# Attention with top-k MLP on one core: dense output rows, query tiles of 1024 columns, and values' products five blocks behind the scores

## The chip, the cores and the metric

One core of a Trainium2 chip runs the program. The metric is the device time of one execution in microseconds, as the median of several runs. TensorE (PE) multiplies matrices, VectorE (DVE), ScalarE (ACT) and GpSimd (POOL) do the elementwise work, and SyncE (SP) issues nearly all transfers to 16 DMA engines.

## The reference

For each of four batches there are 12288 queries of 128 channels. The keys, which are the values too, are 384 x 32 positions averaged over 4 x 4 windows, which leaves 768, and multiplied by a 128 x 128 matrix. Softmax attention follows. On its output `x` a gate picks the 128 rows of a batch with the highest score, and these rows alone get a small MLP added.

```python
kv_pool = kv.reshape(B, H // r, r, W // r, r, C).mean(axis=(2, 4))
k = v = kv_pool.reshape(B, -1, C) @ w_sr
s = (q @ k.transpose(0, 2, 1)) / sqrt(C)
a = exp(s - s.max(-1)); a /= a.sum(-1) + 1e-09
x = a @ v
scores = x @ w_gate                          # one score for a row
top = argpartition(-scores[b], 128)[:128]
out[b, top] = x[b, top] + sigmoid(scores[b, top]) * (relu(x[b, top] @ w1) @ w2)
```

## The kernel before, in words

The loop of lines 602 to 646 goes over 192 blocks of 256 queries, 48 for a batch. Each query of a block is split into a high and a low part, each probability too, so that products in fast formats keep the precision.

Iteration `i` does this. `s_max(i)` (L338) takes the maximum of block i's scores in PSUM on DVE. `AV` (L374) multiplies the turned probabilities of block `i - LAG`, with `LAG` 4, by the values: 36 matmuls of 130 columns, of which 128 are the value, one is the sum of the probabilities and one the gate's score. `S(i + 1)` (L326) makes the next block's scores in 12 matmuls, in the other of two PSUM buffers. `exp` and `to_high` on ACT and `to_low` on DVE and POOL write the block's probabilities to the tile `hl`, a half in fp16 and a half in bf16. `turn(i, 0)` and `turn(i, 1)` (L371) have the DMA engines transpose the two halves into the tile `at`, one DMA for each. `sums`, `recip` and `finish` (L385 to L409) normalise block `i - LAG` on DVE out of the one PSUM tile `o_two`, which the next AV overwrites. `hl` has 4 buffers and `at` has 5.

`finish` multiplies all 130 columns by the reciprocal into the tile `x` (2 blocks, 4 rows of 130 floats in a partition). After each second block POOL copies the gate's column out of `x` to the scores (L406), and SP writes the 128 others to HBM (L408). The four rows lie next to each other in HBM but 130 floats apart in SBUF, so a row of 512 bytes is a piece of its own.

Queries come in through `load_q` (L129): a tile holds 2048 columns (8 blocks), there are two such tiles, and each DMA brings the 512 columns of two blocks, 256 KB. `split_q` (L314) reads the columns two iterations before their scores. `next_keys` (L256) prepares the next batch's keys beside a batch: it loads 1 MB a key tile in two DMAs of 512 KB and sums on POOL. In the last batch there is nothing to prepare. `topk` (L411) and `pick` (L456) select the rows and run the MLP of the batch before, a step at a time at fixed points of the loop.

PE, DVE, ACT and POOL run in the order in which the Python code issues (`InOrder`, L39). SP's DMAs run in one order too, but the scheduler chooses it, and a load stands in it as early as its tile is free. SP's order in the trace repeats every 8 blocks: two transposes a block, an output after each second block, and four query loads, of which three stand next to each other right after a tile of queries has been split for the last time. Key loads come between, alone or in twos.

After the loop (L647 to L735) the last four blocks' products follow, and the last batch's selection and MLP run with nothing beside them.

Of the kernel before, what the change touches and what calls it, by code (L numbers as in the profile page):

```python
# [6 lines left out]
F32 = mybir.dt.float32  # L7
# [7 lines left out]
ALU = mybir.AluOpType  # L15
# [4 lines left out]
P = 128  # L20
B, N, C = 4, 12288, 128
# [4 lines left out]
CHUNK = 2048  # L26
JPC = CHUNK // P
NCH = N // CHUNK
QT = 2
BLK = QT * P  # L30
NBLK = N // BLK
BPC = CHUNK // BLK
VC = C + 2
NCOL = N // P
CUT = 2 * M - HALF
# [29 lines left out]
def attention_topk_mlp(ctx, tc, a, outs, capacity):  # L65
    nc = tc.nc
    pe, dve, act, pool = (InOrder(tc, e) for e in (nc.tensor, nc.vector, nc.scalar, nc.gpsimd))
# [3 lines left out]
    kvp = ctx.enter_context(tc.tile_pool(name="kvp", bufs=3))  # L71
    kvs = ctx.enter_context(tc.tile_pool(name="kvs", bufs=2))
    keys = ctx.enter_context(tc.tile_pool(name="keys", bufs=2))
    qp = ctx.enter_context(tc.tile_pool(name="qp", bufs=2))
    qs = ctx.enter_context(tc.tile_pool(name="qs", bufs=3))
    wk = ctx.enter_context(tc.tile_pool(name="wk", bufs=3))
    hlp = ctx.enter_context(tc.tile_pool(name="hlp", bufs=4))
    at = ctx.enter_context(tc.tile_pool(name="at", bufs=5))
    ob = ctx.enter_context(tc.tile_pool(name="ob", bufs=3))
    sm = ctx.enter_context(tc.tile_pool(name="sm", bufs=4))  # L80
    tk = ctx.enter_context(tc.tile_pool(name="tk", bufs=2))
# [18 lines left out]
    o_two = ps_o.tile([P, QT, 512], F32, name="o_two")  # L100
    o_all = o_two[:, :, 0:VC]
    banks = [o_two[:, j] for j in range(QT)]
# [23 lines left out]

    qraw = {}

    def load_q(b, ch, lo=0, hi=CHUNK):  # L129
        if (b, ch) not in qraw:  # L130
            qraw[b, ch] = qp.tile([P, CHUNK], F32, name="q_raw")
        nc.sync.dma_start(out=qraw[b, ch][:, lo:hi], in_=a["q"][:, b, ch, lo:hi])

    kvset = {}

    def new_keys(b):
        kvset[b] = {
            "kh": keys.tile([P, M], F32R, name="kh"),
            "kl": keys.tile([P, M], F32R, name="kl"),
            "raw": keys.tile([P, KT, 2, P], F32, name="kv_proj"),  # L140
            "vw": keys.tile([P, KT], F32, name="vw"),
            "mx": keys.tile([P, 4], F32, name="mx"),
            "vx": keys.tile([P, 2, KT, VC], F16, name="vx"),
            "sg": keys.tile([P, 4], F32, name="sg"),
        }

    def project(pooled, ps):
        pe.matmul(ps[:, 0], w_k, pooled, start=True, stop=True)
        pe.matmul(ps[:, 1], pooled, w_sr, start=True, stop=True)
# [24 lines left out]
    def v_split(b):  # L174
# [18 lines left out]
        dve.tensor_scalar(out=sg[:, 3:4], in0=sg[:, 0:1], scalar1=float(TAPS), scalar2=None, op0=ALU.mult)  # L193
        vw3, col = vw.rearrange("p (t o) -> p t o", o=1), slice(C + 1, VC)
        act.activation(vw3, vw3, AF.Copy, scale=sg[:, 1:2])
# [14 lines left out]
    def first_keys():  # L210
        new_keys(0)
        load_q(0, 0, 0, 2 * BLK)
        raws = [load_kv(0, kc) for kc in range(3)]
        nc.sync.dma_start(out=cst, in_=a["cst"])
        raws += [load_kv(0, kc, 2) for kc in range(3, KT)]
        load_q(0, 0, 2 * BLK, CHUNK)
        split_q(0, 0)
        kv = kvset[0]
        for kc in range(KT):
            pooled = kvs.tile([P, P], F32, name="pooled")  # L220
            for h in range(2):
                dve.tensor_reduce(out=pooled[:, h * P // 2:(h + 1) * P // 2], in_=raws[kc][:, h], axis=AX.X, op=ALU.add)
            if kc == 4:
                dve.tensor_copy(tri16, tri)
            if kc > 1:
                v_gate(0, kc - 2)
            if kc == 3:
                v_max(0, 0)
            ps = banks[kc % 2][:, 0:2 * P].rearrange("p (a b) -> p a b", a=2)
            if kc < KT - 1:  # L230
                project(pooled, ps)
                act.copy(kv["raw"][:, kc], ps)
                split_k(0, kc, kc + 1, 0)
                split_k(0, kc, kc + 1, 1)
            else:
                warm(4, banks[0][:, 0:P])
                project(pooled, ps)
                kh, kl = (kv[k][:, kc * P:(kc + 1) * P] for k in ("kh", "kl"))
                dve.tensor_copy(kh, ps[:, 0])
                dve.tensor_tensor(out=kl, in0=ps[:, 0], in1=kh.bitcast(F32), op=ALU.subtract)  # L240
                act.copy(kv["raw"][:, kc, 1], ps[:, 1])
                warm(8, banks[1][:, 0:P])
        S(0)
        S(1)
# [64 lines left out]
    scores = {}  # L309
    qsplit = {}  # L310
    st = {}
    xt_ = {}

    def split_q(b, blk):  # L314
        ch, h = divmod(blk, BPC)
        raw = qraw[b, ch][:, h * BLK:(h + 2) * BLK]
        qh = qs.tile([P, 2 * BLK], F32R, name="qh")
        ql = qs.tile([P, 2 * BLK], F32R, name="ql")
        act.copy(qh, raw)
        pool.tensor_tensor(out=ql, in0=raw, in1=qh.bitcast(F32), op=ALU.subtract)  # L320
        for i in range(2):
            qsplit[b, blk + i] = qh[:, i * BLK:(i + 1) * BLK], ql[:, i * BLK:(i + 1) * BLK]

    blocks = [(b, blk) for b in range(B) for blk in range(NBLK)]
# [67 lines left out]
    def recip(n):  # L392
        dve.reciprocal(st[n]["rz"], st[n]["rz"])

    def finish(n):
        b, blk = blocks[n]
        o, rz = st[n]["o"], st[n]["rz"]
        if blk % 2 == 0:
            xt_[b] = ob.tile([P, 2 * QT, VC], F32, name="x")
        x = xt_[b]  # L400
        dve.tensor_tensor(out=x[:, (blk % 2) * QT:(blk % 2 + 1) * QT], in0=o, in1=rz.rearrange("p (j o) -> p j o", o=1).broadcast_to([P, QT, VC]), op=ALU.mult)
        if blk % 2:
            if blk == 1 and b not in scores:
                scores[b] = tk.tile([P, NCOL], F32, name="sc")
            if n < nb - 1:
                pool.tensor_copy(scores[b][:, (blk - 1) * QT:(blk + 1) * QT], x[:, :, C + 1])  # L406
            ch, h = divmod(blk // 2, BPC // 2)
            nc.sync.dma_start(out=outs[b].rearrange("(h p j) d -> h p j d", p=P, j=JPC)[ch, :, h * 2 * QT:(h + 1) * 2 * QT], in_=x[:, :, 0:C])  # L408
        del st[n]  # L409

    def topk(b):  # L411
# [165 lines left out]
    blocks = [(b, blk) for b in range(B) for blk in range(NBLK)]  # L577
# [20 lines left out]

    start(vals, first_values())
    nb = len(blocks)  # L600
    LAG = 4
    for i in range(nb):
        old = i >= LAG
        b, blk = blocks[i]
        if blk % 2 == 0 and i + BPC < nb:
            nb_, nblk = blocks[i + BPC]
            load_q(nb_, nblk // BPC, nblk % BPC * BLK, (nblk % BPC + 2) * BLK)
        if blk == 0 and b + 1 < B:
            start(prep, next_keys(b + 1))
        if i:  # L610
            borrow(s_flat[(i - 1) % 2], s_flat[(i - 1) % 2][:, 512:513])
        s_max(i)
        if old:
            AV(i - LAG, 0)
            at_point("pe")
            AV(i - LAG, 1)
        else:
            at_point("pe")
            warm(18 if i == 0 else 36, banks[0][:, 0:P])
        if i % 2 == 0 and i + 2 < nb:  # L620
            split_q(*blocks[i + 2])
        at_point("ev")
        at_point("up")
        at_point("t")
        at_point("cmp")
        at_point("g")
        if 0 < i < nb - 1:
            S(i + 1, (3, 2, 1, 0))
        exp(i, 1)
        exp(i, 2)  # L630
        to_high(i, 1)
        if old:
            sums(i - LAG)
            recip(i - LAG)
            finish(i - LAG)
        to_low(i, 1, dve)
        exp(i, 0)
        to_high(i, 0)
        turn(i, 0)
        to_low(i, 0, pool)  # L640
        turn(i, 1)
        at_point("d")
        if i in (1, 2):
            advance(vals, "d")
        if old and blocks[i - LAG][1] == NBLK - 1:
            start(select, topk(blocks[i - LAG][0]))
    ended.append(True)  # L647
    room["select"], room["count"] = banks[1][:, VC:VC + HALF], banks[1][:, VC + HALF:VC + HALF + 1]
    n = nb - 1
    b = blocks[n][0]  # L650
    spare = [s_buf[(n + 1) % 2][:, 2 * k:2 * k + 2].rearrange("p k q -> p (k q)")[:, 0:QT * VC].rearrange("p (j c) -> p j c", j=QT) for k in range(3)]
    dest = {n - 3: o_all, n - 2: spare[0], n - 1: spare[1], n: spare[2]}

    def out(m):
        for j in range(QT):
# [2 lines left out]
    def norm(m):  # L658
        sums(m)
        recip(m)  # L660

    def put(m):
        finish(m)
# [7 lines left out]
    sc = scores[b]  # L671
# [4 lines left out]
    for j in range(3):  # L676
        pool.memset(jt[:, j:j + 1], float(j + 1))

    for m in (n - 3, n - 2):
        out(m)  # L680
        norm(m)
        put(m)
    out(n - 1)
    out(n)
    key_part(0, NCOL - 2 * QT)
    for m in (n - 1, n):
        norm(m)
        lo = blocks[m][1] * QT
        dve.tensor_tensor(out=sc[:, lo:lo + QT], in0=st[m]["o"][:, :, C + 1], in1=st[m]["rz"], op=ALU.mult)
        put(m)  # L690
    key_part(NCOL - 2 * QT, NCOL)
    dve.tensor_copy(low, key.bitcast(U16).rearrange("p (n h) -> p n h", h=2)[:, :, 0])
# [74 lines left out]
```

## Time and profile before

| | |
|---|---|
| median of 3 runs | 1020.61 us (1020.28 to 1025.73) |
| the profiled execution: its own time | 1024.38 us |
| the profiled execution: its span in the trace | 1022.6 us |
| granted TensorE clock, mean | 0.963 |
| busy share of PE, PE's weight loads, DVE, ACT, POOL | 88%, 78%, 69%, 75%, 74% |
| DMA traffic | 230 MB, mean 225 GB/s |

The durations below come from the one profiled execution, which is 3.77 us above the median. Its time lies 1.8 us above its span. SP has no busy share on the page, because an instruction that issues a DMA isn't counted as busy; in the timeline it has a start and a duration. In the rows a tile's name stands without its buffer's number, `out<-in`; nearly all instructions bear the line of the helper that records them (L51), so the tiles tell them apart. `at<-hl` is a transpose, `o_two<-vx,at` the products with the values, `s<-...` the scores, `out<-x` an output, `q_raw` and `kv_raw` the loads.

### The profile page before, as it was taken

The page shows a single profiled execution, that of the slowest core. Times are in us where ns is not written, and L with a number is a line of the kernel's source. Part 1 is how long each engine was busy: PE and PEld are TensorE (multiplying, and loading weights), DVE is VectorE, ACT ScalarE, POOL GpSimd, SP SyncE. Part 2 cuts the span into 40 slices and gives each one's busy share as a digit, 9 for nine tenths or more (in the row PEclk, how much of TensorE's full clock was granted, in tenths as well). Part 3 has the DMA queues.
Part 4 walks back from the last instruction along what each step waited for, and adds up shares of the span by engine and source line. Part 5 has one row for each costly group of instructions (what it writes and reads, how often), then busy time and mean ns, then how long its engine had stood idle before and what let it go on. Part 6 is the DMA issues. An engine that isn't in the chain of part 4 may idle for free.

```text
span 1022.6 us, 25609 instructions
## 1 busy us (share of the span) xinstructions
PE 904.1 (88%) x9779; PEld 794.8 (78%) x9779; DVE 705.4 (69%) x1732; ACT 768.6 (75%) x1168; POOL 752.3 (74%) x573
## 2 busy tenths in 40 slices
PE   3899888898999989899999989999999999999616
PEld 2788777787887878778788878888879888888615
DVE  6557555555777767677766766787776788888581
ACT  2678777777887868778797867898888888888400
POOL 1579779867798877688788877999777777777401
PEclk9989999999999999999999999999999999999957
DMA  9899999999999999999999999999999999999800
GB/s 361 212 228 220 244 232 249 229 234 238 241 238 231 242 236 238 241 242 244 232 231 240 233 232 243 244 248 207 245 215 234 227 241 236 235 239 228 182 3 8
DMA packets 674234, 230.15 MB, mean 225 GB/s; under 512 B 606016, under 2 KB 656320, under 8 KB 673344
## 3 DMA queue, kind: packets, MB, share of 16 engines
q1 hardware_dynamic: 673856, 228.00, 109.8%
q8 instruction: 77, 1.26, 0.5%
q0 software_dynamic: 256, 0.52, 0.2%
q14 instruction: 45, 0.37, 0.1%
HBM read 52.04 MB, written 25.43 MB: 76 GB/s over the span
## 4 chain that ended last, share of the span: by engine, by line
PE 46%; DMA 15%; DVE 14%; ACT 14%; issue 6%; POOL 4%; SPq 0%; POOLq 0%; DVEq 0%; ACTq 0%
PE s L51 25%; PE o_two L51 21%; DMA at<-hl 14%; DVE m L51 8%; ACT am L51 6%; ACT hl L51 4%; ACT s L51 2%; POOL hl L51 2%; DVE junk L51 1%; POOL kv_sum L51 1%; POOL ql L51 1%; DMA kv_raw<-in_kv 1%; DVE hl L51 1%; DVE pooled L51 1%; ACT kv_proj L51 1%
## 5 line engine op out<-in xcount | busy, mean ns | idle before, releaser
L51 POOL TENSOR_TENSOR hl<-am,hl 128x1280 bf16<-128x1280 f32 x192 | 505.8, 2634 | 172.8 <-ACT hl L51 99.0
L51 PEld LDWEIGHTS <-at 128*128 128x128 f16 (+1 forms) x6912 | 407.9, 98 | 118.5 <-DMA at<-hl 64.0
L51 PE MATMUL o_two<-vx,at 128*128 128x130 f16 x6804 | 447.7, 222 | 52.5 <-DMA at<-hl 44.4
L51 ACT ACTIVATE am<-s,m 128x512 f32<-128x512 f32 (+1 forms) x384 | 307.0, 799 | 118.1 <-DVE m L51 66.7
L51 DVE TENSOR_REDUCE m<-s 128x2 f32<-128x1536 f32 x192 | 337.2, 1756 | 80.4 <-PE s L51 79.9
L51 PE MATMUL s<-kh,qh 128*128 128x512 f32 (+1 forms) x768 | 278.8, 363 | 8.2 <-DVE rz L51 4.3
L51 PE MATMUL s<-kh,ql 128*128 128x512 f32 (+1 forms) x768 | 260.8, 340 | 0.9 <-POOL ql L51 0.9
L51 PE MATMUL s<-kl,qh 128*128 128x512 f32 (+1 forms) x768 | 260.5, 339 | 0.0
L51 ACT CAST hl<-am 128x1280 f16<-128x1280 f32 x192 | 242.0, 1260 | 6.1
L51 PEld LDWEIGHTS s<-kh,qh 128*128 128x128 f32 x768 | 146.2, 190 | 19.8 <-ACT s L51 5.3
L51 PEld LDWEIGHTS s<-kh,ql 128*128 128x128 f32 x768 | 145.9, 190 | 18.6 <-POOL ql L51 2.5
L51 PEld LDWEIGHTS s<-kl,qh 128*128 128x128 f32 x768 | 147.4, 192 | 8.8
L51 DVE TENSOR_TENSOR hl<-s,hl 128x256 bf16<-128x256 f32 x192 | 81.2, 423 | 79.1 <-ACT hl L51 72.9
L51 POOL TENSOR_TENSOR ql<-q_raw,qh 128x512 fp32r<-128x512 f32 x96 | 122.8, 1279 | 6.7 <-ACT qh L51 6.6
L51 ACT ACTIVATE s<-s,m 128x256 f32<-128x256 f32 x192 | 86.1, 448 | 6.3
L51 DVE TENSOR_TENSOR x<-o_two,rz 128x260 f32<-128x260 f32 x189 | 81.0, 429 | 6.4
L51 DVE TENSOR_SCALAR rz<-o_two,sg 128x2 f32<-128x2 f32 x189 | 41.1, 217 | 59.9 <-PE o_two L51 59.6
L51 ACT CAST hl<-s 128x256 f16<-128x256 f32 x192 | 71.7, 373 | 6.6 <-DMA at<-hl 0.4
L51 ACT CAST qh<-q_raw 128x512 fp32r<-128x512 f32 x96 | 59.1, 615 | 1.1 <-DMA q_raw<-in_q 1.1
L51 POOL TENSOR_TENSOR kv_sum<-kv_raw 128x256 f32<-128x256 f32 x72 | 52.7, 731 | 0.0
L51 PEld LDWEIGHTS <-ones 128*128 128x128 bf16 (+1 forms) x291 | 23.6, 107 | 22.8 <-issue 19.1
L51 PE MATMUL s<-cnt,ones 128*128 128x1 bf16 (+1 forms) x111 | 18.4, 166 | 23.2 <-DVE junk L51 22.9
(163 smaller groups left out, 458.5 us busy)
## 6 DMA issues: line engine op xcount, KB each, us to landing
out<-x SPq DMA_DIRECT2D x96, 256.0 KB, 3.0
q_raw<-in_q SPq DMA_DIRECT2D x93, 256.0 KB, 3.8
kv_raw<-in_kv SPq DMA_DIRECT2D x36, 512.0 KB, 5.1
kv_raw<-in_kv SPq DMA_DIRECT2D x6, 1024.0 KB, 8.8
at<-hl SPq DMA_TRANSPOSE x384, 4.6
w<-in_w SPq DMA_DIRECT2D x2, 512.0 KB
q_raw<-in_q SPq DMA_DIRECT2D x1, 768.0 KB, 7.0
cst<-in_cst SPq DMA_DIRECT2D x1, 320.0 KB
```

The source lines that it names most:

```text
L51: r = f(*args, **kwargs)
```

## The change

Output rows stand dense in `x` (4 rows of 128 floats), and the gate's column goes from PSUM to the scores by an operation of its own on DVE for each block, `gate`, ahead of `finish`; POOL's copy goes. A tile of queries holds 1024 columns and comes in one DMA of 512 KB, issued every fourth block for the blocks 8 to 11 later; there are three such tiles. `LAG` is 5, with 6 buffers of `at`; five blocks follow after the loop, the first and the last of them in `o_two`.

```diff
+QB = 4
-    qp = ctx.enter_context(tc.tile_pool(name="qp", bufs=2))
+    qp = ctx.enter_context(tc.tile_pool(name="qp", bufs=3))
-    at = ctx.enter_context(tc.tile_pool(name="at", bufs=5))
+    at = ctx.enter_context(tc.tile_pool(name="at", bufs=6))
...
-    def load_q(b, ch, lo=0, hi=CHUNK):
-        if (b, ch) not in qraw:
-            qraw[b, ch] = qp.tile([P, CHUNK], F32, name="q_raw")
-        nc.sync.dma_start(out=qraw[b, ch][:, lo:hi], in_=a["q"][:, b, ch, lo:hi])
+    def load_q(b, part, lo=0, hi=QB * BLK):
+        if (b, part) not in qraw:
+            qraw[b, part] = qp.tile([P, QB * BLK], F32, name="q_raw")
+        ch, off = divmod(part * QB * BLK, CHUNK)
+        nc.sync.dma_start(out=qraw[b, part][:, lo:hi], in_=a["q"][:, b, ch, off + lo:off + hi])
...
+    def gate(n):
+        b, blk = blocks[n]
+        if blk == 0:
+            scores[b] = tk.tile([P, NCOL], F32, name="sc")
+        dve.tensor_tensor(out=scores[b][:, blk * QT:(blk + 1) * QT], in0=st[n]["o"][:, :, C + 1], in1=st[n]["rz"], op=ALU.mult)
...
-            xt_[b] = ob.tile([P, 2 * QT, VC], F32, name="x")
+            xt_[b] = ob.tile([P, 2 * QT, C], F32, name="x")
-        dve.tensor_tensor(out=x[:, ...], in0=o, in1=rz...broadcast_to([P, QT, VC]), op=ALU.mult)
+        dve.tensor_tensor(out=x[:, ...], in0=o[:, :, 0:C], in1=rz...broadcast_to([P, QT, C]), op=ALU.mult)
         if blk % 2:
-            if n < nb - 1:
-                pool.tensor_copy(scores[b][:, (blk - 1) * QT:(blk + 1) * QT], x[:, :, C + 1])
-            nc.sync.dma_start(out=outs[b].rearrange("(h p j) d -> h p j d", ...)[...], in_=x[:, :, 0:C])
+            nc.sync.dma_start(out=outs[b].rearrange("(h p j) d -> h p (j d)", ...)[...], in_=x.rearrange("p j d -> p (j d)"))
...
-    LAG = 4
+    LAG = 5
-        if blk % 2 == 0 and i + BPC < nb:
-            nb_, nblk = blocks[i + BPC]
-            load_q(nb_, nblk // BPC, nblk % BPC * BLK, (nblk % BPC + 2) * BLK)
+        if blk % QB == 0 and i + 2 * QB < nb:
+            load_q(blocks[i + 2 * QB][0], blocks[i + 2 * QB][1] // QB)
...
             recip(i - LAG)
+            gate(i - LAG)
             finish(i - LAG)
...
-    dest = {n - 3: o_all, n - 2: spare[0], n - 1: spare[1], n: spare[2]}
+    dest = {n - 4: o_all, n - 3: spare[0], n - 2: spare[1], n - 1: spare[2], n: o_all}
```

## Rows read from the trace of the kernel before

**Rows 1.** The page, part 1: busy time of each engine, share of the span, instructions.

```profile
PE 904.1 (88%) x9779; PEld 794.8 (78%) x9779; DVE 705.4 (69%) x1732; ACT 768.6 (75%) x1168; POOL 752.3 (74%) x573
```

**Rows 2.** Four stretches: us, busy us (instructions) of each engine, clock, DMA share, GB/s.

```profile
60.00:260.00 200.00, 180.94 (x1931) 158.99 (x1929) 120.84 (x216) 154.91 (x229) 157.41 (x119) 0.97 1.18 235
300.00:500.00 200.00, 180.54 (x1979) 157.64 (x1978) 145.81 (x361) 155.87 (x234) 161.53 (x122) 0.98 1.18 240
545.00:645.00 100.00, 92.07 (x995) 81.08 (x994) 71.51 (x174) 77.89 (x115) 80.22 (x62) 0.97 1.19 237
660.00:960.00 300.00, 293.01 (x3332) 260.93 (x3332) 232.91 (x553) 259.98 (x388) 235.79 (x160) 0.99 1.19 232
```

**Rows 3.** Waits of PE over the span: us in total, times, longest.

```profile
PE o_two L51 <- DMA at<-hl: 44.4, 50, 3.0
...
PE o_two L51 <- POOL vx L51: 4.0, 3, 2.2
```

**Rows 4.** The same of the stretch from 770 to 970 us.

```profile
PE o_two L51 <- DMA at<-hl: 1.4, 2, 1.0
```

**Rows 5.** Timeline of SP, 601 to 622 us: start, us, what, how many merged.

```profile
601.04 7.72 SPq L372 DMA_TRANSPOSE at<-hl  x4
608.86 0.53 SPq L408 DMA_DIRECT2D out<-x  x1
609.49 3.07 SPq L372 DMA_TRANSPOSE at<-hl  x2
612.66 1.03 SPq L124 DMA_DIRECT2D kv_raw<-in_kv  x2
613.79 7.16 SPq L372 DMA_TRANSPOSE at<-hl  x2
621.04 0.53 SPq L408 DMA_DIRECT2D out<-x  x1
```

**Rows 6.** Timeline of POOL: the low half of a block's probabilities, near 590 and 290 us.

```profile
589.15 2.63 POOL L51 TENSOR_TENSOR hl<-am,hl 128x1280 bf16<-128x1280 f32 x1 [0.81 <-ACT hl L51]
...
289.92 2.65 POOL L51 TENSOR_TENSOR hl<-am,hl 128x1280 bf16<-128x1280 f32 x1
```

**Rows 7.** Timeline of SP near 290 us.

```profile
289.35 4.63 SPq L372 DMA_TRANSPOSE at<-hl  x3
```

**Rows 8.** DMA packets of short stretches: 568 to 569, 622.6 to 623.2, 660.7 to 664.1.

```profile
DMA packets 1135, 0.29 MB, mean 291 GB/s; under 512 B 1135, under 2 KB 1135, under 8 KB 1135
...
DMA packets 410, 0.21 MB, mean 350 GB/s; under 512 B 0, under 2 KB 410, under 8 KB 410
...
DMA packets 779, 0.87 MB, mean 255 GB/s; under 512 B 395, under 2 KB 395, under 8 KB 779
```

**Rows 9.** DMA packets: 72.7 to 75.6, 204.4 to 208.9, 8 to 19.

```profile
DMA packets 555, 0.62 MB, mean 215 GB/s; under 512 B 427, under 2 KB 427, under 8 KB 555
...
DMA packets 699, 1.15 MB, mean 256 GB/s; under 512 B 443, under 2 KB 443, under 8 KB 699
...
DMA packets 1119, 4.54 MB, mean 413 GB/s; under 512 B 126, under 2 KB 126, under 8 KB 955
```

**Rows 10.** Groups by shape: busy us, mean ns | idle us before, releaser.

```profile
L51 DVE TENSOR_TENSOR x<-o_two,rz 128x260 f32<-128x260 f32 x189 | 81.0, 429 | 6.4
L51 POOL COPY sc<-x 128x4 f32<-128x4 f32 x95 | 18.2, 191 | 18.3 <-DVE x L51 18.2
L51 DVE TENSOR_TENSOR sc<-s,rz 128x2 f32<-128x2 f32 x2 | 0.3, 159 | 0.1
```

**Rows 11.** Timeline, 880 to 887 us: the normalising of a block, and the next AV.

```profile
880.76 0.43 DVE L51 TENSOR_TENSOR x<-o_two,rz 128x260 f32<-128x260 f32 x1
...
882.26 2.23 PE L51 MATMUL o_two<-vx,at 128*128 128x130 f16 x36
```

**Rows 12.** Waits of ACT over the span.

```profile
ACT hl L51 <- DMA at<-hl: 0.4, 1, 0.4
```

**Rows 13.** The page, part 6: DMA issues.

```profile
q_raw<-in_q SPq DMA_DIRECT2D x93, 256.0 KB, 3.8
```

More of the change, by code (lines that the diff above doesn't have):

```diff
@@ L215, in first_keys @@
         raws += [load_kv(0, kc, 2) for kc in range(3, KT)]
-        load_q(0, 0, 2 * BLK, CHUNK)
+        load_q(0, 0, 2 * BLK)
+        load_q(0, 1)
         split_q(0, 0)
@@ L314, in split_q @@
     def split_q(b, blk):
-        ch, h = divmod(blk, BPC)
-        raw = qraw[b, ch][:, h * BLK:(h + 2) * BLK]
+        part, h = divmod(blk, QB)
+        raw = qraw[b, part][:, h * BLK:(h + 2) * BLK]
         qh = qs.tile([P, 2 * BLK], F32R, name="qh")
@@ L398, in finish @@
         if blk % 2 == 0:
-            xt_[b] = ob.tile([P, 2 * QT, VC], F32, name="x")
+            xt_[b] = ob.tile([P, 2 * QT, C], F32, name="x")
         x = xt_[b]
-        dve.tensor_tensor(out=x[:, (blk % 2) * QT:(blk % 2 + 1) * QT], in0=o, in1=rz.rearrange("p (j o) -> p j o", o=1).broadcast_to([P, QT, VC]), op=ALU.mult)
+        dve.tensor_tensor(out=x[:, (blk % 2) * QT:(blk % 2 + 1) * QT], in0=o[:, :, 0:C], in1=rz.rearrange("p (j o) -> p j o", o=1).broadcast_to([P, QT, C]), op=ALU.mult)
         if blk % 2:
-            if blk == 1 and b not in scores:
-                scores[b] = tk.tile([P, NCOL], F32, name="sc")
-            if n < nb - 1:
-                pool.tensor_copy(scores[b][:, (blk - 1) * QT:(blk + 1) * QT], x[:, :, C + 1])
             ch, h = divmod(blk // 2, BPC // 2)
-            nc.sync.dma_start(out=outs[b].rearrange("(h p j) d -> h p j d", p=P, j=JPC)[ch, :, h * 2 * QT:(h + 1) * 2 * QT], in_=x[:, :, 0:C])
+            nc.sync.dma_start(out=outs[b].rearrange("(h p j) d -> h p (j d)", p=P, j=JPC)[ch, :, h * 2 * QT * C:(h + 1) * 2 * QT * C], in_=x.rearrange("p j d -> p (j d)"))
         del st[n]
@@ L677, in attention_topk_mlp @@
         pool.memset(jt[:, j:j + 1], float(j + 1))
-    for m in (n - 3, n - 2):
+    for m in range(n - LAG + 1, n - 1):
         out(m)
         norm(m)
+        gate(m)
         put(m)
@@ L687, in attention_topk_mlp @@
         norm(m)
-        lo = blocks[m][1] * QT
-        dve.tensor_tensor(out=sc[:, lo:lo + QT], in0=st[m]["o"][:, :, C + 1], in1=st[m]["rz"], op=ALU.mult)
+        gate(m)
         put(m)
```

## The prediction

> **What bounds the kernel now.** I read the busy shares first, then the same by stretches, then PE's waits, then SP's timeline. PE is busy 88% of the span and the other engines 69% to 78% [rows 1], so none is full over the whole. The stretches differ, though. A block has 48 large matmuls (12 for scores, 36 for values). By the counts of matmuls, about 40 and 41 blocks fall into the 200 us from 60 and from 300 on and 21 into the 100 us from 545 on, some 4.9 us a block; from 660 to 960 it is 69 blocks in 300 us, 4.32 us a block with PE busy 98% [rows 2]. So PE is the bound late in the run and something else is before that.
>
> The waits name it: PE waits 44.4 us for the transposed tiles `at` [rows 3], and only 1.4 us of that lies between 770 and 970 us [rows 4]. But a transpose waits for its own data, or it stands in a queue, and these ask for different cures. SP's timeline tells which. From 601.04 us each DMA's issue begins within 0.1 us of the end of the one before [rows 5]: SP never sleeps, and it is the issue itself that grows. Two transposes take 3.07 us in one row and 7.16 us in the next, behind two key loads: the queue is full and pushes back. POOL ends the low half of a block at 589.15 + 2.63 = 591.78 us [rows 6]; counted through in order, its transpose is the second of SP's four from 601.04 us, issued at 602.6 us. It stood in the queue for 10.8 us. Near 290 us the same half ends at 292.57 us [rows 6], when the third transpose of SP's row from 289.35 to 293.98 us begins [rows 7]: there the queue had caught up. Reading SP's whole timeline this way, the queue is behind in three stretches, roughly 60 to 260, 300 to 500 and 545 to 645 us, 500 us or some 102 blocks; in the others PE sets the pace.
>
> **Prices in the queue.** The DMA packets of short stretches give them; packets of 256 bytes are transposes, so their count over 1135 in a us [rows 8] is the time that transposes took of a stretch. A transpose (1536 packets) is 1.35 us. An output runs at 350 GB/s, so 256 KB take 0.75 us [rows 8]. Three query loads of 256 KB took 3.4 us less 395/1135 = 0.35 us, so 1.02 us each [rows 8]. A key load of 512 KB alone took 2.9 less 0.38 = 2.52 us; two behind one another 4.5 less 0.39, so 2.05 us each; before the first transpose, loads run at 413 GB/s, which makes 1.27 us of 512 KB [rows 9].
>
> **The change part by part.** The sum goes against the profiled execution's 1024.4 us, which is 3.8 us above the median.
>
> Dense output: 96 DMAs of 512 pieces of 512 bytes become 96 of 128 pieces of 2 KB. No output of such pieces is in the trace. The bounds are loads: at best 413 GB/s, 0.63 us, so -0.12 us; at worst the query loads' 1.02 us, +0.27 us. I take -0.08, near the lower end, because the output's row shows no start-up loss as the loads' do. In the stretches in which the queue is behind there are 51: -4 us (-6 to +14). The Trainium skill (DMA: Bandwidth & Descriptors, section Specifications) says that pieces from 512 bytes on already run at line rate. By that rule the term is 0 and the sum -5.5 in place of -9.5; rows 8 and 9, 350 against 413 GB/s, disagree a little.
>
> Query loads: two of 256 KB become one of 512 KB every fourth block (93 and a first one become 47 or so [rows 13]). Two cost 2.03 us now. One costs between 1.27 us and the lone key load's 2.52. I take 2.3, nearer the upper end: it has the same size and the same pieces of 4 KB, and it will mostly stand alone between transposes, as each smaller tile is freed by itself. That is +0.27 us for each of 25 in the stretches: +6.5 us (-19 to +12). SP issues 47 DMAs less, some 0.5 us each by the length of an output's issue [rows 5]; while SP issues, the queue works off what is in it, so 0 (to -12).
>
> LAG 5: a block's transposes may land one block later before PE has to wait. That adds nothing to the queue's rate. It lets PE run one block further ahead in each stretch in which the queue is behind, and the queue makes it up in the stretch after. Three stretches at most 4.32 us each are 13 us; I take 10, because `hl`, with 4 buffers as before, comes next: ACT rewrites it four blocks later, and where it now waits 0.4 us in all [rows 12] it will begin to wait. Bounds: 0, if `hl` stops it at once, and -44.4, all of PE's wait. At the start PE's first AV waits in all 4.0 us for the values' halves `vx` [rows 3]; one iteration more covers that, but the queue is full of loads then: -2 us (0 to -4). After the loop there is one AV more, 2.23 us [rows 11], and one fewer ahead of the last scores; the last transposes land later than it ends: 0 (+2 to -2).
>
> Gate: 192 operations of 159 ns on DVE [rows 10] are +30.5 us busy; the normalising of 256 columns in place of 260 gives back 4/260 of 81.0 us. Behind the gate on DVE stand `x` and `to_low`; PE's next AV waits for `x` to free `o_two`. `x` ends at 880.76 + 0.43 = 881.19 and that AV starts at 882.26, with the scores' matmuls between [rows 11]: 1.07 us of cover for 0.16 to 0.2 us, so 0. Without cover it would be 189 x 0.2 = +38 us. POOL's copies go, -18.2 us busy, with the 18.3 us that POOL waited for `x` ahead of them [rows 10]. POOL's next work is the low half, whose transpose stands in the queue anyway, or isn't waited for where PE sets the pace: 0 (to -18).
>
> Sum: -4 + 6.5 - 10 - 2 = -9.5, so 1024.4 - 9.5 = 1014.9 us for an execution like the profiled one, and 1011 for the median.
>
> **The rivals.** First, only the queue's rate counts: `hl` stops PE where `at` did, or the stretches are too long for one block of lead to matter. Then -4 + 6.5, 1023 us. For it: SP never idle for 100 us on end. Against: the three times that the queue caught up.
>
> Second, slower: the 512 KB query load is dearer than a key load. Its first pieces come with nothing read ahead, and all transposes behind it on SP's queue wait. The lone key load's whole stretch is 2.9 us, transposes included; at that price all 47 loads, if the queue then stays behind throughout, cost 47 x 0.87 = +41, less the 16 us of the other terms: 1046 us; in the three stretches alone 25 x 0.87 = +22, less 16: 1027. I write 1033. It decides from 2.03 + 16/25 = 2.67 us a load. For it: pairs of small loads, 1.02 us each, are cheaper than any key load after the start. Against: two key loads in a row cost 2.05 us each.
>
> Third, much faster: all 44.4 us of waits for `at` go, 976 us. Against it stands SP's full timeline.
>
> Fourth, faster by the loads: 512 KB at the start's 1.27 us, 25 x -0.76 = -19, with the other -16: 986 us. The Trainium skill (DMA: Bandwidth & Descriptors, section Rules for kernel authors) advises to merge transfers into larger ones, which would have it so; the key loads in mid-run, 215 and 256 GB/s against 255 GB/s with the small ones, show no such gain.
>
> **How the numbers follow.** A measurement here can tell about 0.5%, 5 us. The forecast has 0.34, the first rival 0.26, the second 0.2, the third and fourth 0.1 each. Faster is forecast, third and fourth, 0.54; same the first, 0.26; slower the second, 0.2. The range of 8 in 10 reaches from 980 us (most of the fourth, the edge of the third) to 1036 (the second as written). The forecast's own range is 1000 to 1020.
>
> **What would show it.** Right: PE's wait for `at` well below 44.4 us, a wait of ACT for `hl` in its place, and the blocks before 645 us below 4.9 us each. The output's window above 350 GB/s. Query loads near 2.3 us less their transposes. Wrong: waits for `at` as before, or SP's rows of transposes longer behind query loads; `x` ending after the next AV could start; a PE share below 98% after 660 us.

## The result and the profile after

The changed kernel took 1033.16 us (median of 4, 1029.66 to 1034.78) beside 1023.09 us of the kernel before: 1.0101 times as long, with an interval from 1.0071 to 1.0131. The forecast of a faster kernel was wrong; the time lies in the range, where the second rival had it. The profiled execution took 1029.66 us, the shortest of the four; that of the kernel before took 1024.38 us, a little above its median.

First the page, part 1, of the changed kernel, which answers to [rows 1]:

```profile
PE 907.2 (88%) x9815; PEld 793.8 (77%) x9815; DVE 705.7 (69%) x1922; ACT 764.7 (74%) x1168; POOL 739.4 (72%) x478
```

The shares say nothing. The stretches of [rows 2] do (us, busy us and instructions of each engine, clock, DMA share, GB/s), of the changed kernel:

```profile
60.00:260.00 200.00, 184.47 (x1982) 160.49 (x1982) 123.51 (x266) 156.88 (x234) 159.89 (x104) 0.97 1.15 239
300.00:500.00 200.00, 173.33 (x1841) 149.08 (x1839) 135.28 (x377) 144.79 (x219) 150.19 (x97) 0.97 1.16 232
545.00:645.00 100.00, 93.96 (x1025) 81.86 (x1025) 71.98 (x199) 79.28 (x118) 82.07 (x55) 1.00 1.18 237
660.00:960.00 300.00, 291.13 (x3317) 259.01 (x3315) 232.81 (x620) 259.35 (x388) 229.96 (x125) 1.00 1.19 231
```

From 60 to 260 us PE did 51 matmuls more than before, about one block; from 300 to 500 us 138 fewer, about three; from 545 to 645 us 30 more, a little over half a block. In the last stretch PE stays at 97%. So it is the queue's stretches that changed, two for the better and one for the worse, and hardly PE's.

The waits of PE and of ACT in the changed kernel, answering to [rows 3, 12]:

```profile
PE o_two L52 <- DMA at<-hl: 20.4, 23, 2.6
```

```profile
ACT hl L52 <- DMA at<-hl: 92.8, 56, 4.9
```

PE waits 24 us less for `at`. ACT, which hardly ever waited to rewrite `hl`, now stands still for 92.8 us until a transpose has read it. The wait changed hands.

Last, the end. The row of `m` gives the last maximum of the loop (the second of the two times), the row of `low` the moment when the last selection's keys are complete. Of the kernel before:

```profile
L51 DVE TENSOR_REDUCE m<-s x192: 1741/1758/1759, 29.7 to 952.4; 128x2 f32<-128x1536 f32 x192
...
L51 DVE COPY low<-key x1: 202/202/202, 968.8 to 968.8; 128x96 uint16<-128x96 uint16 x1
```

Of the changed kernel:

```profile
L52 DVE TENSOR_REDUCE m<-s x192: 1741/1757/1759, 29.2 to 953.1; 128x2 f32<-128x1536 f32 x192
...
L52 DVE COPY low<-key x1: 203/203/203, 970.7 to 970.7; 128x96 uint16<-128x96 uint16 x1
```

With spans of 1022.6 and 1027.9 us, the part after the last maximum grew from 70.2 to 74.8 us: 4.6 of the 5.3 us between these two executions arise after the loop, of which 1.2 lie before `low`. So in this pair the loop lost only 0.7 us. The medians are 10 us apart; the other 5 us lie, in all likelihood, in the loop of other executions, but no trace shows that.

### The profile page after: what moved, and what is told of

It is laid out like the page before. It is cut to its first block, busy times and chain, and to the rows that moved or that the text cites. A ratio compares the mean times of both kernels' runs of the same rounds, so it can differ in the third digit from the quotient of the medians.

```text
span 1027.9 us, 25755 instructions
## 1 busy us (share of the span) xinstructions
PE 907.2 (88%) x9815; PEld 793.8 (77%) x9815; DVE 705.7 (69%) x1922; ACT 764.7 (74%) x1168; POOL 739.4 (72%) x478
## 4 chain that ended last, share of the span: by engine, by line
DMA 29%; PE 26%; DVE 18%; ACT 13%; issue 7%; POOL 6%; SPq 1%; POOLq 0%; DVEq 0%; ACTq 0%
DMA at<-hl 27%; PE s L52 15%; PE o_two L52 11%; DVE m L52 9%; ACT am L52 5%; ACT hl L52 5%; POOL hl L52 3%; ACT s L52 2%; DVE hl L52 2%; POOL ql L52 2%; DVE junk L52 2%; POOL kv_sum L52 1%; SPq L375 1%; DMA kv_raw<-in_kv 1%; DVE pooled L52 1%
## 5 line engine op out<-in xcount | busy, mean ns | idle before, releaser
L52 PEld LDWEIGHTS <-at 128*128 128x128 f16 (+1 forms) x6912 | 401.6, 97 | 88.5 <-issue 61.2
L52 PE MATMUL o_two<-vx,at 128*128 128x130 f16 x6804 | 440.0, 220 | 25.4 <-DMA at<-hl 20.4
L52 ACT CAST hl<-s 128x256 f16<-128x256 f32 x192 | 71.6, 373 | 97.3 <-DMA at<-hl 92.8
L52 DVE TENSOR_TENSOR x<-o_two,rz 128x256 f32<-128x256 f32 x189 | 78.4, 415 | 0.0
L52 PEld LDWEIGHTS <-ones 128*128 128x128 bf16 x327 | 25.6, 106 | 28.6 <-issue 19.7
```

Source lines behind the costliest of these rows:

```text
L52: r = f(*args, **kwargs)
```

## The experiments

Ratios are to the kernel before on the same chip, with the interval; its median was 1017 to 1027 us, by the chip. "Queue price" is read from the DMA records: the time from the moment when nine tenths of one transpose's packets have begun to the same moment of the next, between 66 and 745 us and without an instruction fetch, as a median. With nothing between them that is 1.46 us. What stands between them adds to it. A price on the queue is not yet a change of the kernel's time.

### Each part by itself

**Dense output and gate alone,** with LAG 4 and the loads of before:

```diff
-            xt_[b] = ob.tile([P, 2 * QT, VC], F32, name="x")
+            xt_[b] = ob.tile([P, 2 * QT, C], F32, name="x")
...
+            gate(i - LAG)
```

> The kernel before with the dense output and the separate gate alone (query loads of 256 KB, values' products four blocks behind). Theory A, each part by its own price: in the trace after, an output between two transposes costs the queue 0.66 us where before it cost 0.83, so 0.17 us on each of 51 to 96 outputs is saved, 9 to 16 us at the most and half of it where only the stretches that the queue binds count: 1023 becomes 1011 to 1018. Theory B, the dense rows do nothing for the time (the prediction's rival on the queue's rate): 1021 to 1025. Theory C, the gate on VectorE costs more than the copies on GpSimd saved: over 1026.

Measured: 0.9953 (0.9930 to 0.9976), 1013.54 us. An output adds 0.80 us to the queue before (32 spacings) and 0.64 after (19). Two spacings with an output, of the kernel before and of the changed kernel, by their DMA packets (an output of 512-byte pieces is the 512 packets from 512 bytes to 2 KB, a dense one the 128 of 2 KB and more):

```profile
DMA packets 2094, 0.66 MB, mean 294 GB/s; under 512 B 1582, under 2 KB 2094, under 8 KB 2094
```

```profile
DMA packets 1711, 0.66 MB, mean 315 GB/s; under 512 B 1583, under 2 KB 1583, under 8 KB 1711
```

The same bytes take 2.08 us where they took 2.23. Theory A holds at the lesser of its values, and the rival without any gain is out. At 0.16 us an output, the 51 outputs in the three stretches would be 8 us; 2 to 7 us of time came of it.

**Query loads of 512 KB alone,** with LAG 4 and the old output:

```diff
-        if blk % 2 == 0 and i + BPC < nb:
...
+        if blk % QB == 0 and i + 2 * QB < nb:
+            load_q(blocks[i + 2 * QB][0], blocks[i + 2 * QB][1] // QB)
```

> The kernel before with the query tiles of 1024 columns and their single 512-KB loads alone. Theory A, the loads are what made the change slower: in the trace after, a 512-KB query load between two transposes takes the queue about 2.7 us where two of 256 KB took 1.9, so 25 loads in the stretches that the queue binds lose 20 us and the time is 1035 to 1048. Theory B, the prediction's price (2.3 for 2.03): 1026 to 1033. Theory C, the loads are hidden and the later products are to blame: 1021 to 1025.

Measured: 1.0077 (1.0048 to 1.0106), 1024.94 us, in the range that theory B gave for the time. The price is theory A's, though: a load alone adds 2.65 us to a spacing (21) where the prediction had 2.3. At 2.65 for 2.03 the 25 loads would cost 15.5 us; half of that shows. That the loads are hidden is out.

**LAG 5 alone** (with the query tiles of 1024 columns, which make room for the sixth buffer of `at`, filled by loads of 256 KB):

```diff
-    at = ctx.enter_context(tc.tile_pool(name="at", bufs=5))
+    at = ctx.enter_context(tc.tile_pool(name="at", bufs=6))
-    LAG = 4
+    LAG = 5
```

> The kernel before with the values' products five blocks behind alone (at with 6 buffers; query tiles of 1024 columns with 3 buffers, only so that the sixth buffer has room, filled by the same 256-KB loads at the same blocks as before; output and gate as before). Theory A, the lag costs in the tail and returns little in the loop: the key of the last selection and the selection of batch 2 that runs beside it each come a block later, 1.9 and 3.4 us by the two traces, and in the loop ScalarE waits for hl in place of TensorE for at, 0 to 8 us won: 1020 to 1028. Theory B, the prediction's: no cost in the tail and 10 us won in the loop: 1009 to 1016.

Measured: 1.0023 (0.9997 to 1.0050), 1020.89 us: theory A. PE's and ACT's waits:

```profile
PE o_two L52 <- DMA at<-hl: 15.6, 17, 2.0
```

```profile
ACT hl L52 <- DMA at<-hl: 65.2, 42, 5.2
```

The wait changes hands with the lag alone, and 10 us do not come of it. One thing else changed with the smaller tiles: on SP's queue the loads of 256 KB now stand mostly in pairs beside an output (35 pairs), where the kernel before mostly has three in a row; a load in such a pair adds 1.18 us to a spacing (18), one of three 1.04 (8). The pair of runs with LAG 4 and 5 further down has no such difference and says the same.

**The change with the loads of before:**

```diff
-        if blk % QB == 0 and i + 2 * QB < nb:
-            load_q(blocks[i + 2 * QB][0], blocks[i + 2 * QB][1] // QB)
+        if blk % 2 == 0 and i + 2 * QB < nb:
+            nb_, nblk = blocks[i + 2 * QB]
+            load_q(nb_, nblk // QB, nblk % QB * BLK, (nblk % QB + 2) * BLK)
```

> The changed kernel with the query loads of before: each tile of 1024 columns is filled by two loads of 256 KB, two blocks apart. Theory A, the loads made the change slower: 1008 to 1019, that is at least 14 us under the changed kernel and under the kernel before. Theory C, the later products made it slower: still 1029 or more.

Measured: 0.9958 (0.9936 to 0.9979), 1013.75 us. Without the 512-KB loads the change is faster than the kernel before. SP's order is not that of the kernel before here either: it is that of the run above, and but for one load at the start that of the two loads back to back below (0.9930), so those two runs measure nearly the same kernel twice.

### The loads in company

Alone the parts make 0.9953 x 1.0077 x 1.0023 = 1.0053, and the whole has 1.0101. The intervals of the three parts and of the whole together leave about half a per cent, so this rest is not clear of the noise. Five runs looked for it. With LAG 4 outputs fall to odd blocks and with LAG 5 to even ones, where the loads stand.

**Dense output and 512-KB loads with LAG 4:**

```diff
-    LAG = 5
+    LAG = 4
```

> The changed kernel with the values' products four blocks behind again (at 5 buffers): dense output and 512-KB query loads together. Theory A, the parts add: 0.9953 by 1.0077 is 1.003 of the kernel before (1.000 to 1.006). Then the changed kernel's 1.0101 has a surplus that only the lag with the wide loads makes. Theory B, the surplus is between the wide loads and the dense output that stands beside them: 1.008 or more.

Measured: 1.0016 (0.9992 to 1.0040), as the parts add. On SP's queue all its loads stood apart from the outputs; in the changed kernel 29 of 34 between 66 and 745 us stood beside one (counting those with no key load next to them). A load adds 2.83 us to a spacing here (25).

**The 512-KB load one block later:**

```diff
-        if blk % QB == 0 and i + 2 * QB < nb:
+        if blk % QB == 1 and i + 2 * QB < nb:
```

> The changed kernel with the 512-KB query load issued one block later, in a block without an output (in the changed kernel load and output share a block). Theory A, the load costs by itself: the queue takes 2.7 us for it alone and 3.0 beside an output, so 0.3 us on 25 loads is won: 1.003 to 1.012 of the kernel before. Theory B, the neighbourhood of load and output is what costs: 0.994 to 1.000.

Measured: 1.0060 (1.0028 to 1.0091). But the scheduler, which orders SP's transfers, put 29 of 34 loads back beside an output, so this says nothing of the neighbourhood. It is a second measurement of nearly the changed kernel, and by the two the rest is 0.1% to 0.5%.

**The same, tied:** the load depends in SP's order on the last transpose issued before it.

```diff
+        tc.add_manual_dep(r.ins, turned[-1], ...)
```

> The changed kernel with the 512-KB query load issued one block later and tied behind that block's last transpose, so that on SyncE's queue it really stands alone between two transposes, away from the output. Theory A, the load costs by itself: a load alone took the queue 2.7 us, beside an output 3.0, so 0.3 us on some 30 loads is won, 9 us at the most: 1.000 to 1.009 of the kernel before. Theory B, the neighbourhood is what costs: 0.990 to 0.997.

Measured: 1.0051 (1.0026 to 1.0075). SP's timeline, in the changed kernel and in this run (start, us, what, how many):

```profile
309.00 10.04 SPq L375 DMA_TRANSPOSE at<-hl  x4
319.13 0.53 SPq L134 DMA_DIRECT2D q_raw<-in_q  x1
319.75 0.41 SPq L413 DMA_DIRECT2D out<-x  x1
320.26 8.33 SPq L375 DMA_TRANSPOSE at<-hl  x4
```

```profile
333.28 3.91 SPq L381 DMA_TRANSPOSE at<-hl  x2
337.24 0.57 SPq L135 DMA_DIRECT2D q_raw<-in_q  x1
337.92 4.67 SPq L381 DMA_TRANSPOSE at<-hl  x2
342.68 0.53 SPq L420 DMA_DIRECT2D out<-x  x1
```

The load now stands alone, and the kernel is still slower than before: theory A. By the medians the neighbourhood accounts for half a per cent at most.

**Two loads of 256 KB back to back,** where the 512-KB load stood beside the output, then tied as above:

```diff
-            load_q(blocks[i + 2 * QB][0], blocks[i + 2 * QB][1] // QB)
+            for h in range(2):
+                load_q(blocks[i + 2 * QB][0], blocks[i + 2 * QB][1] // QB, 2 * h * BLK, 2 * (h + 1) * BLK)
```

> The changed kernel with each 512-KB query load issued as two loads of 256 KB back to back, at the same block: the same bytes at the same moment, in pieces of 2 KB where there were pieces of 4 KB. Theory A, the long pieces of one load are what costs: 0.996 (0.993 to 1.000) of the kernel before, as with the loads of before. Theory B, 512 KB at one moment is what costs, ahead of the transposes behind it: 1.005 to 1.013, as the changed kernel.

> The same, with two loads of 256 KB back to back in place of each load of 512 KB. Two such loads took 1.9 to 2.4 us where they stood alone and 2.4 to 2.6 beside an output. Theory A: a little under the run with the two loads beside the output (0.993), 0.985 to 0.993. Theory B, their place makes no difference any more: 0.990 to 0.996.

Measured: 0.9930 (0.9904 to 0.9957) beside the output and 0.9934 (0.9910 to 0.9959) apart from it. The same bytes at the same place cost 1.2% less in two transfers (0.9934 against 1.0051), and the place makes no difference. So the cause lies in the load itself: in its being one transfer. One spacing of either tied run, one load and then two:

```profile
DMA packets 1720, 0.92 MB, mean 219 GB/s; under 512 B 1592, under 2 KB 1592, under 8 KB 1720
```

```profile
DMA packets 1862, 0.92 MB, mean 258 GB/s; under 512 B 1606, under 2 KB 1606, under 8 KB 1862
```

0.92 MB, a transpose and 512 KB of queries, take 4.20 us as one load and 3.56 us as two.

### Does `hl` hold the lag back?

**Loads of 256 KB one at a time into tiles of 512 columns, and `hl` with 5 buffers:**

```diff
-QB = 4
+QB = 2
-    qp = ctx.enter_context(tc.tile_pool(name="qp", bufs=3))
+    qp = ctx.enter_context(tc.tile_pool(name="qp", bufs=4))
-    hlp = ctx.enter_context(tc.tile_pool(name="hlp", bufs=4))
+    hlp = ctx.enter_context(tc.tile_pool(name="hlp", bufs=5))
```

> Dense output and five blocks behind, query loads of 256 KB into tiles of 512 columns (4 buffers), and hl with 5 buffers (hs of the selection with one buffer, which makes the room). Theory A, hl's 4 buffers take back what the lag wins in the loop (ScalarE waited 68 us for hl in the run with these loads and 4 buffers): ScalarE's wait falls to under 25 us and the time to 0.985 to 0.992 of the kernel before. Theory B, the queue's own rate binds and a deeper hl only lengthens the line: ScalarE's wait falls, another takes its place, and the time stays at 0.994 to 0.998.

Measured: 1.0094 (1.0061 to 1.0126). ACT's wait for `hl` fell to 7.6 us, but the loads had changed with it: single ones beside an output added about 1.6 us each (36 spacings), so 3.2 a pair. So this run does not tell what `hl` does; the next has the loads of before.

**The change with the loads of before, and `hl` with 5 buffers:**

```diff
-    hlp = ctx.enter_context(tc.tile_pool(name="hlp", bufs=4))
+    hlp = ctx.enter_context(tc.tile_pool(name="hlp", bufs=5))
```

> Dense output, five blocks behind and the query loads of before (0.9958), with hl at 5 buffers and the same order of the loads on SyncE's queue (four tiles of the selection have one buffer each, which makes the room). Theory A, hl's 4 buffers take back what the lag wins, and the slow run with 5 buffers was due to its loads of 256 KB standing one by one beside every output (1.6 us each): 0.982 to 0.992. Theory B, the queue's rate binds, and a deeper hl only moves the wait from ScalarE back to TensorE: 0.993 to 0.999. Theory C, a deeper hl is harmful in itself: 1.003 or more.

Measured: 0.9999 (0.9973 to 1.0024), against 0.9958 with 4 buffers. PE's wait with 4 buffers, then with 5:

```profile
PE o_two L52 <- DMA at<-hl: 16.2, 17, 2.0
```

```profile
PE o_two L52 <- DMA at<-hl: 44.8, 52, 2.9
```

And ACT's, in the same order:

```profile
ACT hl L52 <- DMA at<-hl: 68.4, 44, 5.6
```

```profile
ACT hl L52 <- DMA at<-hl: 5.6, 5, 2.7
```

Theory B, at its upper end or past it. ACT is freed, PE waits 44.8 us for `at` as it did at first, and nothing is won. So `hl` was not what held the lag's gain back; its wait only showed where the line behind the queue ended. Two reservations: the fifth buffer's room was taken from the selection, four of whose tiles have one buffer here in place of two, and what that costs by itself was not measured; and of the loss against 4 buffers a part lies at the end, where the stretch after the last maximum takes 78.3 us for 73.9 in the profiled executions.

### What of the load is dear?

One transfer in pieces of 2 KB (the rows laid out in two halves in device memory), and two transfers of 64 partitions in pieces of 4 KB, both tied:

```diff
+        nc.sync.dma_start(out=w_[:, d], in_=a["q"][:, b, d, part])
```

```diff
+            for h in range(2):
+                load_q(blocks[i + 2 * QB][0], blocks[i + 2 * QB][1] // QB, p0=64 * h, p1=64 * (h + 1))
```

> The tied 512-KB query load as one transfer again, but in pieces of 2 KB (the query rows laid out in device memory so that the two halves of a tile lie apart). Theory A, the length of the pieces costs: as with two loads of 256 KB, 2.1 us of the queue and 0.990 to 0.997 of the kernel before. Theory B, the size of the transfer costs: 2.75 us and 1.003 to 1.008.

> The tied query load as two transfers of 256 KB that take 64 partitions each, in pieces of 4 KB. Theory A, the length of the pieces: 2.7 us of the queue for the two and 1.003 to 1.008. Theory B, the size of the transfer: 2.1 us and 0.990 to 0.997. Over 1.01, if transfers of 64 partitions are dear by themselves.

Measured: 1.0045 (1.0017 to 1.0073) and 1.0030 (1.0005 to 1.0055). The first speaks against the theory that the length of the pieces costs (theory A of either run), the second against the theory that the size of the transfer does: short pieces alone do not help, and two transfers alone help little. A spacing of the run with short pieces, 4.33 us for the same 0.92 MB:

```profile
DMA packets 1846, 0.92 MB, mean 212 GB/s; under 512 B 1590, under 2 KB 1590, under 8 KB 1846
```

Four loads of 128 KB in pieces of 1 KB, tied; and the best kernel (below) with the 36 later key loads cut in two as well:

```diff
+            for h in range(4):
+                load_q(blocks[i + 2 * QB][0], blocks[i + 2 * QB][1] // QB, h * BLK, (h + 1) * BLK)
```

```diff
+                for lo in range(0, P // 2, P // 2 if b == 0 else P // 4):
...
+                    nc.sync.dma_start(out=t[:, i * n:(i + 1) * n, k], in_=a["kv"][:, b, kc, i * n:(i + 1) * n, k])
```

> The tied query load as four transfers of 128 KB back to back, in pieces of 1 KB. Theory A, what costs is how much of one transfer each DMA engine has to begin with, so four are at least as cheap as two: the four take the queue 2.1 us or less and the time is 0.986 to 0.995 of the kernel before. Theory B, each transfer has a price of its own, and two are the best: 2.4 us or more and 0.996 to 1.003.

> The run with two tied query loads and the shorter end (0.9878), and each later key load of 512 KB (36 of them, 4-KB pieces) cut into two transfers of 256 KB in pieces of 2 KB as well. Theory A, the price is one of loads in general: 0.6 us less for each of 36 key loads, of which the queue's bound stretches hold most: 0.975 to 0.984. Theory B, it is particular to the query loads, or the keys' order on the queue gives it back: 0.986 to 0.992.

Measured: 1.0116 (1.0083 to 1.0148), worse than one load and outside both theories, though the price is near theory B's, so smaller is not always better; and 0.9872 (0.9842 to 0.9902) against 0.9878, no gain from the keys that can be told. There too the price fell: a spacing with an output and 512 KB of keys takes 4.85 us (7) with one load and 4.28 (7) with two. A lower price need not show in the time. Together, with a second reading beside the spacings: a fit of the time of each six transposes in a row, to so much a transpose, an output, a query load, a key load and an instruction fetch (stretches of 66 to 745 us without a pause of SP over 0.6 us; for 512 KB of queries uncertain by 0.3 to 0.4 us):

| 512 KB of queries as | median spacing, us (count) | less 1.46 | by the fit | ratio |
|---|---|---|---|---|
| one load, 4-KB pieces, tied | 4.21 (24) | 2.75 | 2.48 | 1.0051 |
| one load, 2-KB pieces, tied | 4.33 (24) | 2.87 | 2.61 | 1.0045 |
| two of 64 partitions, tied | 4.15 (26) | 2.69 | 2.32 | 1.0030 |
| four of 128 KB, tied | 3.85 (24) | 2.39 | 2.44 | 1.0116 |
| two of 256 KB, tied | 3.56 (21) | 2.10 | 2.08 | 0.9934 |

The two loads of 256 KB over all partitions are cheapest by each reading, clearly by the spacings; the fit's differences are no larger than its uncertainty. The fit's 0.4 us less than one load would be 13 us on some 33 loads between 66 and 745 us, the spacings' 0.65 us would be 21; the ratios differ by 12. Why, stays open, and so does the time of the four loads, slower than their price.

### The end, and what the lag is worth

Two loads beside the output, with the selection of batch 2 taken a step further in each step of the last batch's first search (one execution, for its trace):

```diff
             advance(select)
+            if name == "th2":
+                advance(select)
```

> The run with two loads of 256 KB beside the output, and the selection of batch 2 taken forward twice instead of once in each of the first 8 steps of the last selection. Theory A, the lag costs the end 3.4 us because batch 2's selection ends a block later and its gather and products stand in line behind the last search: from the last copy to low to the end 53 to 55 us, where the kernels with five blocks behind took 56 to 58.6 and those with four 53.4 to 54. Rival, the end is longer for another reason: still 56 or more.

The rows of `m` and `low`:

```profile
L52 DVE TENSOR_REDUCE m<-s x192: 1739/1756/1759, 29.7 to 937.4; 128x2 f32<-128x1536 f32 x192
...
L52 DVE COPY low<-key x1: 201/201/201, 954.9 to 954.9; 128x96 uint16<-128x96 uint16 x1
```

GpSimd's timeline (start, us, what, idle time before it and its releaser), of which the two gathers, the first of them batch 2's:

```profile
973.81 0.97 POOL L52 DMA_INDIRECT xe<-out,idx  x1 [28.08 <-DVE base L52]
...
996.30 0.97 POOL L52 DMA_INDIRECT xe<-out,idx  x1 [2.21 <-DVE idx L52]
```

The same gathers of the kernel before, and of the changed kernel:

```profile
992.53 1.00 POOL L51 DMA_INDIRECT xe<-out,idx  x1 [31.39 <-DVE base L51]
...
1010.56 0.97 POOL L51 DMA_INDIRECT xe<-out,idx  x1 [2.26 <-DVE idx L51]
```

```profile
997.66 0.97 POOL L52 DMA_INDIRECT xe<-out,idx  x1 [36.14 <-DVE idx L52]
...
1016.13 0.97 POOL L52 DMA_INDIRECT xe<-out,idx  x1 [2.21 <-DVE idx L52]
```

Batch 2's gather comes 23.7 us after `low` starts in the kernel before, 27.0 in the changed kernel, and 18.9 with the extra steps; the end follows 53.8, 57.2 and 53.1 us after `low` (span 1008.0 us). So theory A: with LAG 5 the selection of batch 2 begins a block later, its gather waits until the last search is over (it is released by its own `idx`, where before a step of the search, `base`, stood last), and its MLP stands in front of the last one's. The other traces agree: batch 2's gather comes 23.7 or 23.8 us after `low` in all five with LAG 4, 26.9 or 27.0 in all twelve with LAG 5, and 18.9 in the three with the extra steps; the stretch after the last maximum takes 69.2 to 70.5, 73.9 to 78.3, and 70.7 to 71.1 us.

The tied pair with the extra steps, and the tied pair with LAG 4, where it stands at `blk % QB == 0`:

> Two loads of 256 KB tied away from the output (0.9934) and the selection of batch 2 taken forward twice in each of the first 8 steps of the last search, which shortened the stretch after the loop by 4.1 us in the run beside the output: 0.987 to 0.992, the lowest so far. Rival, the stretch after the loop is shorter but the loop takes it back: 0.993.

> The same two loads of 256 KB, away from the output, with the values' products four blocks behind (at 5 buffers). Theory A, the lag wins nothing where the queue's rate binds and costs 4.6 us at the end: 0.986 to 0.991, below the same with five. Theory B, the lag wins 8 us or more in the loop: 0.996 or more.

Measured: 0.9878 (0.9837 to 0.9919), 1008.28 us, and 0.9932 (0.9906 to 0.9957). The second equals the tied pair with LAG 5 (0.9934). The rows of `m` of the tied pair with LAG 5 (span 1006.8 us), then with LAG 4 (1006.6 us):

```profile
L52 DVE TENSOR_REDUCE m<-s x192: 1742/1757/1759, 29.6 to 931.9; 128x2 f32<-128x1536 f32 x192
```

```profile
L52 DVE TENSOR_REDUCE m<-s x192: 1742/1758/1760, 30.2 to 936.3; 128x2 f32<-128x1536 f32 x192
```

From the last maximum to the end the one with LAG 4 took 70.3 us against 74.9, and from the first maximum to the last 906.1 against 902.3 us, in one execution of each: by this pair the lag won some 4 us in the loop and gave them back after it; the ratios leave 3 to 4 us either way. That lies between the two theories. The shorter end adds to it: dense rows, pairs of 256 KB, LAG 5 and the extra steps make the kernel that beats both. LAG 4 with the extra steps was not run.

This run and the one with dense output and 512-KB loads (1.0016) differ in the load alone: both have LAG 4, and SP's order is the same but for the first and the last of the loads. One load in place of two costs 1.0016 less 0.9932, 9 us.

## Why the prediction was wrong

**What bounds the kernel** held: the queue in the early stretches, PE after them. In the profiled pair two of the three stretches named gained and one lost; the loop as a whole lost 0.7 us, and 4.6 us came after it.

**Dense output**, -4 us with a saving of 0.08 each on 51: near in time, 1019 x -0.0047 = -4.8 us, but by two errors that cancel, which is luck: it saved 0.16 us each, twice the forecast, and about half of the 8 us on the queue reached the time of the run that had it (with the gate). The rule of the Trainium skill (DMA: Bandwidth & Descriptors, section Specifications), line rate from pieces of 512 bytes on, would have it at 0; the measured 2.23 against 2.08 us speaks against it here.

**Query loads**, +6.5 us at 2.3 a load: alone +7.8 us, near again, and again by luck. The price was 2.65 us, so the term was mis-sized (25 x 0.62 is 15.5 us), and half of it reached the time, where the sum counts every us of the queue in full. At the same place on the queue, one load for two costs 9 us with LAG 4, 12 us with LAG 5 apart from the outputs (1.0051 less 0.9934), and 10 to 17 us with LAG 5 beside them (1.0060 and 1.0101 less 0.9930 and 0.9958), each uncertain by some 4 us. So with the lag the load may cost more of the time; against 9 us, only the larger of these values are clear of the noise. Their price on the queue does not change with the lag: by the spacings it is 2.65 and 2.83 us with LAG 4, and 2.75 with LAG 5 where it stands alone. The second rival had 2.67 as the price from which it decides, and its place, loads on the queue ahead of the transposes; the time came out as it said, and it was given 0.2. Its number, 1033, is luck in part: it counts on 16 us of gains from the other terms, of which only the 4.8 of the dense output came. The Trainium skill's rule to merge transfers (DMA: Bandwidth & Descriptors, section Rules for kernel authors) fails here from 256 to 512 KB: merged, 512 KB cost more. From four of 128 KB to two of 256 KB it holds in the time, 1.0116 against 0.9934.

**LAG 5**, -10 us, is the step that failed: +2.3 us alone, with the interval from -0.3 to +5.1, and nothing in the pair with LAG 4 and 5. The wait for `hl` came as foreseen; the error was to think that a block of lead is worth 3 x 4.32 us less a little. In the changed kernel PE's wait fell by 24 us and ACT's rose by 92; a buffer more for `hl` turned such a shift round and won nothing. The sentence of the first rival, that only the queue's rate counts, was nearly right; some 4 us are won in the loop, by one pair of executions.

**After the loop**, 0: +4.6 us. I costed the AV and the landing of the transposes (1.2 us of the 4.6 come before `low`) and left out `select`, which starts on `old`, a block later, and whose steps after the loop stand in one line with the last search. The diff does not touch it; the lag does.

**The start**, -2: PE's wait for `vx` fell from 4.0 to 1.6 us; a gain in time cannot be told apart from the lag's. **The gate**, 0: right; it takes 159 ns and `x` 415 ns, and PE's share after 660 us is 97% as against 98%.

In the sum, the terms measured alone give -4.8 + 7.8 + 2.3 = +5.3 us where I had -9.5; the whole has +7 to +13 by the interval. Of the 20 us between forecast and result, 14 are the lag with its start and end (-12 forecast, +2.3 measured); 1 is the load alone, less 1 for the dense output; the other 5 arise only when the parts are together, are not clear of the noise, and stay unexplained.

## What to carry to other kernels

Where an in-order transfer queue binds, slack in buffers only decides which engine stands still; look for what each transfer costs the queue, and try the sizes, since a merged load can be dearer than two. Do not count a price on the queue in full: here about half of it reached the time. When a stage is moved by an iteration, follow everything that is started from its index, down to the work after the loop, and see which iterations its transfers now share with others. And before reading an experiment on the order of transfers, look in its trace whether the order changed.

## What the runs showed of the hardware

Around an instruction fetch the transposes almost stop. In the kernel before, two transposes with nothing between them are 1.45 us apart (142 spacings), but 2.86 us when an instruction fetch falls in between (30). The DMA engines' busy share (tenths, in 40 slices) and packets of 564 to 567 us of the kernel before, in which one did:

```profile
DMA  9999999999999999090000001001000105990999
...
DMA packets 1560, 0.41 MB, mean 136 GB/s; under 512 B 1559, under 2 KB 1559, under 8 KB 1559
## 3 DMA queue, kind: packets, MB, share of 16 engines
q1 hardware_dynamic: 1559, 0.39, 135.4%
q8 instruction: 1, 0.02, 2.2%
```

1559 packets in 3 us are 520 in a us, where transposes run at 1135 [rows 8], and for some 1.2 us of the three the 16 engines are nearly idle, so the fetch does not crowd the transposes out by its own bytes (one packet, 16 KB). Why they stop is not shown. The fit gives 1.0 to 1.6 us a fetch, and there are 77 of them in either kernel: some 80 to 120 us of the queue's time that no step of the prediction looked at. No run here removed a fetch, so what one costs in the kernel's time is not shown.
